# Two loads under way instead of four, a new instruction order, and 256-wide filling products in a fused RWKV-attention and SwiGLU kernel

## The chip, the cores and the metric

The kernel runs on one core of one Trainium2 chip. The metric is the device time in microseconds of one launch; the time before is the median of three runs. A profiled execution of the same kernel gives the rows that are quoted below. All times without a unit are microseconds, and those of the trace count from the first instruction of the span.

A core has a matrix engine (TensorE, called PE in the rows, with its weight loads as PEld), three engines for elementwise work (VectorE or DVE, ScalarE or ACT, GpSimd or POOL) and SyncE (SP), which in this kernel only issues transfers. An engine works through its instructions in the order in which they stand in its own queue; engines wait for each other by semaphores. TensorE is granted either its full clock or half of it, by a throttle that the profile shows as "PEclk".

## The reference

```python
batch, n_heads, seq, head_dim = (4, 8, 768, 48)
...
for t in range(S):
    kt, vt, rt = (k[:, :, t], v[:, :, t], r[:, :, t])
    cur = np.einsum('bhd,bhe->bhde', u[None] * kt, vt)
    y[:, :, t] = np.einsum('bhd,bhde->bhe', rt, state + cur)
    state = w[None, :, :, None] * state + np.einsum('bhd,bhe->bhde', kt, vt)
...
x = np.ascontiguousarray(attn_out.transpose(0, 2, 1, 3)).reshape(B * S, H * D)
...
rms = np.sqrt(np.mean(x * x, axis=-1, keepdims=True) + 1e-06)
xn = x / rms * rms_g
g = xn @ w_gate
silu = g * (1.0 / (1.0 + np.exp(-g)))
val = xn @ w_val
return (silu * val @ w_out).astype(np.float32)
```

So a linear attention with a decaying state runs over 768 positions for 4 batches of 8 heads of 48 channels, and its 3,072 rows of 384 go through a normalisation and a gated feed-forward layer of width 1,536. The three weight matrices arrive in 64-bit floating point, the rest in 32-bit.

## The kernel before

**Tiling.** The sequence is cut into 12 chunks of 64 positions. A chunk of all four batches is 256 tokens, called stage s (0 to 11). Each stage has a mixing part (attention) and a feed-forward part. Stages 0 and 1 go through the feed-forward layer one by one; from stage 2 on two stages share it, with seven products in place of eight (names f1 to f7, and P1 to P7 for the second layer).

**The names of the operations** (the number behind a name is the stage, and a half of the batches is called half 0 or half 1):

- On SP: *load k*, *load r* (stage 0's keys and receptances, one transfer for each half), *load chan* (both together, later stages, 1,024 KB), *load tok* (the same by tokens, 384 or 768 KB), *load v* (512 KB), *utab* (the bonus u, two transfers), *load 0* to *load 25* (pieces of the weights, 384 KB for the first six and 576 KB for the rest; 0 to 5 are the first quarter of gate and value weights, 6 to 17 the other three, 18 to 25 the output weights), *move* (heads 6 and 7 to their rows, two transfers), *store*, and *look* (the weights once more, for a check of their range).
- A piece of weights is rounded to 32 bits by four operations: *ulp* on ScalarE, *bits1* and *bits2* on VectorE, *sum* on GpSimd. There are six raw buffers and three of each intermediate one.
- On TensorE, for mixing: *E* (r by u times k: the bonus on the diagonal), *A* (r by k, decayed: the scores), *Y* (the outputs), *U* (the update of the state). These are many small products: E, A and U have 64 instructions each, Y has 128; in stage 0 they are done by halves (E and A 32, Y 48 instructions).
- Around them: *ku* (ScalarE, u times k), *R* and *K* (VectorE or GpSimd, r and k decayed), *d* and *m* (VectorE, the diagonal and the masked scores), *sq*, *yT* (ScalarE, squares and outputs), *yb* and *xb* (ScalarE, halves of yT or x exchanged between partitions), *gdup* and *wk* (tables of the decay, made once: gdup on ScalarE, then TensorE, then ScalarE), *h* (VectorE, decayed keys for U), *Rc* and *S*, *E* on ScalarE (copies for the state).
- The normalisation: *r* (TensorE, mean squares, in stages 0 and 1 products one column wide), *ms*, *inv*, *diag* (VectorE) and *pow* (GpSimd), *spread* (TensorE), *rms* (ScalarE), *x* (VectorE).
- The feed-forward part: *g s i o* is one of the two products for stage s, weight quarter i, block o; the first uses the gate-and-value array wa with yT or x, the second wb with yb or xb. Twelve instructions each. *silu*, *gv* and *hm* follow on ScalarE and VectorE; *P s i* is the second layer.

**The order.** All operations are added to a `Plan` (1,536 of them, each with an engine, an estimated cost and what it reads and writes). `ORDER`, a list of 1,536 numbers in the source, says in which order they are given out; `Plan.give` walks it, and each engine's queue follows from it. Dependencies become semaphore waits; the order decides who queues behind whom. `Plan.times` computes due times from the estimated costs, and `give` uses them for one thing: at a gap between TensorE operations it calls `warm(since, until)` with the two due times, and `warm` issues products of a matrix of ones that nobody reads, to fill the gap. A product in 32 bits is two instructions in the trace, with a weight load each.

**The loads under way.** Every input transfer on SP passes through `InOrder.at_most(n, give)`, which appends it to `flying` and, when more than n are in that list, makes the new one wait for the landing of the oldest. The limit is `IN_FLIGHT`, 4. `utab`, `move` and `store` don't pass through it; `look` has a list of its own with a limit of 1. Since SP's queue is in order, a load that waits, for the limit, for a raw buffer or for its target's last reader, holds everything behind it.

Of the kernel before, what the change touches and what calls it, by code (L numbers as in the profile page):

```python
# [49 lines left out]
P = 128  # L50
# [22 lines left out]
def feature_order():  # L73
# [10 lines left out]
    0, 6, 8, 42, 44, 5, 4, 7, 21, 11, 10, 41, 43, 16, 1, 2, 3, 45, 46, 47, 76, 12, 51, 48, 49, 52, 53, 55, 31, 36, 26,  # L84
    13, 14, 58, 50, 59, 15, 54, 17, 22, 60, 62, 65, 66, 100, 18, 19, 23, 24, 113, 9, 108, 103, 20, 67, 68, 83, 56, 27,
    61, 84, 63, 64, 57, 25, 69, 70, 38, 33, 39, 28, 71, 72, 124, 77, 86, 78, 126, 90, 29, 34, 118, 193, 85, 79, 87,
    30, 123, 80, 133, 32, 127, 125, 102, 81, 195, 82, 105, 106, 104, 37, 200, 128, 134, 35, 40, 107, 91, 131, 129,
    109, 114, 95, 130, 132, 92, 135, 119, 73, 110, 136, 96, 137, 155, 115, 111, 120, 116, 205, 210, 121, 139, 140, 97,
    138, 101, 93, 75, 74, 279, 112, 117, 141, 142, 143, 156, 150, 151, 157, 122, 98, 196, 163, 159, 160, 144, 197,
    198, 149, 145, 161, 206, 201, 164, 146, 199, 191, 274, 192, 284, 88, 152, 158, 162, 147, 148, 167, 218, 207, 202,  # L90
    165, 168, 169, 166, 203, 212, 213, 171, 172, 215, 170, 216, 208, 175, 176, 204, 209, 179, 180, 211, 177, 173, 217,
    174, 178, 183, 187, 89, 181, 182, 276, 219, 277, 153, 227, 275, 184, 188, 281, 194, 289, 280, 222, 282, 321, 311,
    306, 185, 225, 189, 247, 248, 249, 186, 214, 154, 190, 99, 278, 283, 251, 252, 255, 285, 250, 253, 254, 220, 256,
    257, 94, 238, 259, 263, 260, 264, 291, 286, 287, 288, 258, 267, 313, 308, 292, 314, 307, 224, 290, 228, 221, 271,
    316, 293, 261, 312, 268, 317, 265, 269, 223, 226, 309, 229, 331, 326, 336, 272, 266, 270, 262, 310, 315, 298, 302,
    294, 295, 242, 230, 322, 233, 234, 328, 355, 352, 318, 323, 299, 303, 296, 231, 300, 304, 297, 232, 353, 356, 235,
    236, 243, 327, 346, 319, 324, 305, 301, 329, 237, 244, 341, 273, 386, 390, 391, 387, 246, 354, 358, 245, 357, 320,
    325, 330, 332, 359, 362, 388, 392, 342, 333, 338, 334, 343, 344, 335, 339, 347, 337, 340, 345, 361, 364, 365, 348,
    360, 389, 375, 407, 349, 380, 363, 383, 381, 239, 393, 384, 500, 350, 366, 406, 394, 395, 351, 368, 369, 416, 437,
    367, 396, 241, 370, 501, 371, 382, 405, 404, 502, 398, 372, 399, 400, 373, 504, 503, 397, 438, 507, 509, 240, 374,  # L100
    376, 408, 378, 512, 377, 401, 402, 445, 409, 410, 385, 403, 413, 439, 446, 456, 457, 417, 441, 440, 447, 411, 442,
    462, 443, 444, 448, 451, 449, 463, 450, 464, 452, 453, 455, 454, 506, 458, 460, 465, 505, 459, 470, 467, 471, 466,
    468, 472, 508, 469, 473, 414, 415, 418, 590, 461, 422, 481, 474, 412, 476, 482, 510, 477, 478, 475, 483, 518, 591,
    513, 480, 484, 489, 485, 511, 479, 486, 490, 491, 487, 514, 488, 628, 492, 627, 519, 515, 520, 525, 493, 495, 624,
    526, 527, 496, 625, 497, 494, 521, 499, 528, 533, 523, 522, 530, 534, 419, 420, 423, 421, 424, 428, 524, 516, 517,
    425, 636, 529, 535, 498, 531, 544, 532, 626, 536, 634, 539, 598, 537, 545, 629, 540, 647, 541, 633, 538, 546, 543,
    547, 552, 635, 549, 548, 542, 550, 551, 630, 553, 631, 555, 554, 558, 632, 556, 563, 559, 560, 562, 565, 564, 557,
    567, 637, 426, 427, 429, 430, 566, 651, 568, 561, 571, 569, 570, 574, 582, 584, 575, 572, 573, 599, 577, 576, 578,
    638, 579, 434, 431, 583, 600, 595, 596, 601, 639, 581, 580, 592, 606, 585, 589, 593, 611, 432, 433, 588, 435, 586,
    602, 603, 587, 597, 436, 607, 642, 612, 643, 700, 640, 594, 747, 644, 701, 608, 615, 645, 756, 641, 652, 609, 610,  # L110
    646, 748, 614, 648, 649, 749, 616, 613, 617, 619, 618, 681, 744, 745, 650, 605, 653, 654, 621, 604, 682, 620, 657,
    746, 622, 683, 623, 660, 826, 689, 656, 684, 655, 685, 754, 690, 757, 753, 751, 691, 686, 706, 687, 688, 692, 695,
    693, 707, 708, 696, 697, 699, 709, 694, 702, 658, 703, 704, 714, 711, 698, 712, 715, 659, 661, 750, 662, 710, 663,
    705, 716, 717, 713, 725, 718, 755, 762, 719, 666, 720, 726, 827, 752, 727, 721, 723, 758, 722, 724, 728, 863, 733,
    860, 730, 664, 665, 763, 734, 729, 731, 732, 667, 669, 735, 736, 759, 760, 739, 864, 737, 769, 740, 771, 861, 741,
    770, 764, 765, 865, 743, 862, 772, 777, 866, 738, 766, 767, 670, 778, 668, 671, 774, 742, 773, 775, 780, 675, 779,
    776, 783, 834, 781, 867, 873, 782, 788, 784, 785, 790, 789, 835, 787, 791, 796, 793, 792, 786, 869, 797, 798, 794,
    795, 799, 802, 883, 800, 870, 676, 807, 803, 804, 806, 809, 808, 810, 801, 815, 812, 672, 673, 674, 677, 816, 768,
    761, 811, 805, 678, 888, 813, 818, 814, 821, 819, 817, 836, 831, 832, 871, 822, 823, 820, 872, 868, 825, 824, 828,
    829, 833, 874, 837, 843, 838, 679, 680, 844, 875, 839, 830, 878, 879, 847, 876, 841, 980, 981, 846, 877, 887, 880,  # L120
    842, 881, 845, 848, 851, 882, 884, 889, 886, 885, 984, 850, 891, 852, 890, 853, 919, 855, 849, 917, 918, 983, 920,
    982, 854, 856, 857, 990, 840, 858, 922, 921, 923, 924, 893, 859, 925, 892, 896, 931, 936, 926, 937, 927, 932, 933,
    928, 942, 929, 935, 944, 943, 945, 986, 938, 985, 939, 894, 930, 940, 934, 993, 895, 947, 950, 998, 987, 951, 946,
    948, 899, 1063, 941, 953, 952, 949, 954, 956, 961, 957, 1096, 958, 963, 962, 960, 964, 988, 992, 955, 965, 966,
    989, 969, 959, 967, 968, 972, 1097, 900, 897, 970, 898, 991, 975, 973, 976, 994, 901, 971, 1098, 905, 1001, 977,
    974, 979, 978, 999, 1005, 1000, 1007, 1006, 1003, 1013, 1008, 1002, 1010, 1009, 1011, 1012, 995, 1102, 1014, 1015,
    1070, 1016, 1019, 1017, 1105, 902, 903, 904, 908, 1062, 1024, 1020, 1021, 1119, 1023, 1026, 1025, 1027, 1018,
    1106, 1028, 1029, 1032, 1022, 1030, 1031, 1035, 1033, 1100, 1034, 1038, 1036, 1043, 1039, 906, 1103, 1040, 1045,
    1044, 1124, 1004, 1037, 909, 907, 911, 996, 1047, 1042, 1046, 1099, 1048, 1041, 1049, 1051, 1071, 1050, 1101,
    1109, 910, 1123, 1054, 1052, 1108, 1104, 1107, 997, 914, 1057, 1055, 1216, 1056, 1110, 1060, 1053, 1058, 1059,  # L130
    1061, 1064, 1072, 1111, 912, 1065, 1114, 1115, 1067, 1068, 1073, 1078, 1074, 1075, 1083, 1172, 1173, 913, 1069,
    1112, 1217, 1066, 1219, 915, 916, 1113, 1116, 1084, 1079, 1117, 1080, 1118, 1120, 1218, 1121, 1122, 1082, 1125,
    1126, 1087, 1229, 1076, 1088, 1086, 1089, 1091, 1085, 1155, 1127, 1153, 1154, 1077, 1128, 1156, 1093, 1094, 1158,
    1157, 1159, 1160, 1220, 1092, 1090, 1081, 1095, 1161, 1167, 1228, 1223, 1162, 1225, 1163, 1164, 1168, 1129, 1169,
    1226, 1165, 1171, 1174, 1221, 1234, 1177, 1299, 1178, 1132, 1180, 1298, 1166, 1222, 1179, 1175, 1176, 1186, 1170,
    1181, 1224, 1227, 1182, 1332, 1183, 1187, 1184, 1185, 1230, 1232, 1130, 1131, 1333, 1188, 1189, 1192, 1190, 1197,
    1193, 1135, 1335, 1194, 1199, 1198, 1235, 1191, 1196, 1200, 1205, 1195, 1202, 1203, 1133, 1134, 1206, 1201, 1138,
    1207, 1208, 1204, 1334, 1211, 1209, 1241, 1212, 1336, 1344, 1231, 1236, 1136, 1213, 1243, 1242, 1210, 1345, 1337,
    1237, 1215, 1244, 1214, 1249, 1238, 1239, 1246, 1245, 1250, 1251, 1247, 1248, 1137, 1139, 1140, 1144, 1252, 1255,
    1253, 1338, 1341, 1254, 1260, 1256, 1257, 1306, 1259, 1262, 1261, 1307, 1263, 1268, 1265, 1258, 1266, 1269, 1264,  # L140
# [18 lines left out]
class InOrder:  # L159


    def __init__(self, tc, engine):
        self.tc, self.engine, self.flying = tc, engine, []
# [87 lines left out]
def fast(ctx, tc, chan, tok, vpad, wka, wkb, wot, cols, u_row, out, bad):  # L251
# [12 lines left out]
    FIRST, IN_FLIGHT = 2, 4  # L264
# [25 lines left out]
    ones = c_tile([P, P], "ones")  # L290
# [85 lines left out]
    def load_chan(s):  # L376
        sp.at_most(IN_FLIGHT, lambda: sp.dma_start(out=CH, in_=chan[s]))
# [1479 lines left out]
```

## Time and profile before

| what | value |
|---|---|
| three runs | 595.24, 594.35, 594.51; median 594.51 |
| the profiled execution, its time | 594.61 |
| its span, first to last instruction | 592.9 |
| transfers | 62.97 MB, 22,766 packets; q1 (SP's) 61.36 MB, q8 (instructions) 0.95 MB in 58 packets |
| TensorE's waits before the tail | issue 1.7 (85.36) and 1.4 (13.49), VectorE 1.1 and 0.8, ScalarE 0.8 and 0.3, a transfer 0.6 |

In the rows of the chain of waits the columns are start, duration, engine and what it writes; "issue" is time in which the engine waited for nothing that the profile shows. All instructions stand on one line of the source, 179, since a helper emits them; so rows are told apart by the tile that is written (bank_a, bank_b, bank_c and at are the four accumulators).

The first 33 of the span are the head: stage 0's and stage 1's mixing with the first feed-forward products between them. TensorE's part of it, as the trace has it (start, name, instructions):

```
 1.15 fill x16          11.49 A 0 (half 0) x32    21.70 fill x4        28.61 A 1 x64
 5.25 E 0 (half 1) x32  12.07 fill x8             22.32 wk x4          29.70 g 0 0 1, wb x12
 5.87 fill x4           13.16 Y 0 x48             22.91 g 0 0 0, wb    31.10 g 0 0 2, wa x12
 6.86 E 0 (half 0) x32  15.71 r 0, r 0 x12        23.69 g 0 0 1, wa    32.49 Y 1 x128
 8.60 A 0 x32           17.14 g 0 0 0, wa, wa x24 24.98 g 0 0 0, wb    34.48 g 0 0 2, wb x12
 9.23 fill x12          19.47 fill x8             25.75 U 0 x64
10.76 Y 0 x48           21.27 spread 0 x2         26.72 E 1 x64
```

### The profile page before, as it was taken

The numbers are of one execution on the slowest core, as the hardware profiler recorded it, in microseconds if no ns is written. First come the engines' busy times: TensorE is split into PE (matmuls) and PEld (weight loads), VectorE is DVE, ScalarE is ACT, GpSimd is POOL, SyncE is SP. The second block draws the span as 40 slices with busy tenths as digits, with TensorE's granted clock in tenths as the row PEclk, the third lists the DMA queues.
The fourth block names the chain that finished last, engine by engine and source line by source line (L and its number), as shares of the span: only waits on it lengthen the run. The fifth ranks groups of instructions, "written<-read, shape, count | busy, mean of one in ns | idle before, by whom it ended". The sixth has DMA issues, their size and how long they took to land.

```text
span 592.9 us, 16578 instructions
## 1 busy us (share of the span) xinstructions
PE 581.5 (98%) x7270; PEld 517.2 (87%) x7270; DVE 416.3 (70%) x622; ACT 293.9 (50%) x713; POOL 41.7 (7%) x40
## 2 busy tenths in 40 slices
PE   7999989999999999999999999999999999999996
PEld 6888877667888999888899888899888899888896
DVE  7788768785786987786785676796766586355642
ACT  5774457374455744464373455594365482124100
POOL 3253234200000000000000000000000000000000
PEclk9899999999999999999999999999999999999999
DMA  8876462321415122523232335301441110301002
GB/s 276 303 249 264 158 248 83 126 61 54 154 65 166 55 74 73 181 84 97 81 92 54 92 108 200 117 24 30 137 157 46 52 63 12 96 3 54 1 4 54
DMA packets 22766, 62.97 MB, mean 106 GB/s; under 512 B 2944, under 2 KB 9760, under 8 KB 21280
## 3 DMA queue, kind: packets, MB, share of 16 engines
q1 hardware_dynamic: 21920, 61.36, 31.6%
q8 instruction: 58, 0.95, 0.7%
q10 hardware_dynamic: 768, 0.49, 0.3%
q14 instruction: 20, 0.16, 0.1%
HBM read 56.04 MB, written 4.72 MB: 102 GB/s over the span
## 4 chain that ended last, share of the span: by engine, by line
PE 96%; ACT 1%; issue 1%; DMA 1%; SPq 0%; DVE 0%; DVEq 0%
PE bank_b L179 33%; PE bank_a L179 27%; PE bank_c L179 27%; PE at L179 8%; DMA chan<-in_chan_dram 1%; ACT ku L179 0%; SPq L179 0%; ACT ST L179 0%; ACT wk L179 0%; DVE chan L179 0%; ACT RX L179 0%; ACT ulp L179 0%; ACT diag L179 0%; DVE rows_out L179 0%; DVE RR L179 0%
## 5 line engine op out<-in xcount | busy, mean ns | idle before, releaser
L179 DVE TENSOR_TENSOR gv<-bank_b,m 128x512 f32<-128x512 f32 x90 | 62.1, 690 | 61.3 <-PE bank_b L179 57.1
L179 ACT ACTIVATE gv<-gv 128x512 f32<-128x512 f32 (+1 forms) x60 | 30.8, 522 | 74.6 <-DVE gv L179 74.5
L179 PE MATMUL bank_b<-xa,wa 64*128 64x256 f32 x444 | 55.2, 379 | 1.7 <-issue 1.7
L179 DVE TENSOR_TENSOR gv<-bank_c,gv 128x512 f32<-128x512 f32 x60 | 41.4, 690 | 21.6 <-PE bank_c L179 21.1
L179 PEld LDWEIGHTS bank_b<-xa,wa 64*128 64x128 f32 x444 | 42.6, 187 | 7.6 <-issue 2.8
L179 PE MATMUL bank_a<-xb,wb 64*128 64x256 f32 x372 | 46.2, 379 | 0.0
L179 PE MATMUL bank_a<-xa,wa 64*128 64x256 f32 x372 | 45.6, 378 | 0.0
L179 PE MATMUL bank_a<-wo,h 128*128 128x192 f32 x264 | 45.2, 327 | 0.0
L179 ACT ACTIVATE MT<-dmask,du 128x64 f32<-128x64 f32 x160 | 41.9, 338 | 6.1 <-DVE du L179 6.0
L179 PE MATMUL bank_b<-t,s 64*128 64x256 f32 x360 | 44.4, 379 | 0.0
L179 PE MATMUL bank_b<-t,wb 64*128 64x256 f32 x360 | 44.2, 378 | 0.0
L179 PE MATMUL bank_c<-t,s 64*128 64x256 f32 x360 | 43.9, 376 | 0.0
L179 PE MATMUL bank_c<-xb,s 64*128 64x256 f32 x360 | 43.9, 376 | 0.0
L179 ACT COPY m<-bank_a 128x512 f32<-128x512 f32 (+1 forms) x35 | 19.9, 568 | 47.8 <-PE bank_a L179 39.1
L179 PEld LDWEIGHTS bank_a<-wo,h 128*128 128x128 f32 x264 | 43.2, 190 | 0.5
L179 ACT ACTIVATE gv<-bank_a 128x256 f32<-128x256 f32 x30 | 11.5, 382 | 57.5 <-PE bank_a L179 57.5
L179 PEld LDWEIGHTS bank_a<-xb,wb 64*128 64x128 f32 x372 | 35.7, 187 | 4.6 <-issue 0.3
L179 PEld LDWEIGHTS bank_a<-xa,wa 64*128 64x128 f32 x372 | 35.8, 187 | 4.2
L179 ACT ACTIVATE rows_out<-rows_out 128x384 f32<-128x384 f32 x72 | 39.1, 556 | 0.5
L179 PEld LDWEIGHTS bank_b<-t,s 64*128 64x128 f32 x360 | 34.4, 187 | 4.7 <-issue 0.7
L179 PEld LDWEIGHTS bank_c<-t,s 64*128 64x128 f32 x360 | 34.9, 187 | 4.0
L179 PEld LDWEIGHTS bank_c<-xb,s 64*128 64x128 f32 x360 | 34.9, 187 | 4.0
(189 smaller groups left out, 1099.0 us busy)
## 6 DMA issues: line engine op xcount, KB each, us to landing
chan<-in_chan_dram SPq DMA_DIRECT2D x11, 1024.0 KB, 5.5
TOK<-in_tok_dram SPq DMA_DIRECT2D x10, 768.0 KB, 4.8
V<-in_vpad_dram SPq DMA_DIRECT2D x12, 512.0 KB, 4.6
raw<-in_wot_dram SPq DMA_DIRECT2D x8, 576.0 KB, 5.5
rows_out<-in_wka_dram SPq DMA_DIRECT2D x12, 384.0 KB, 3.2
rows_out<-in_wkb_dram SPq DMA_DIRECT2D x12, 384.0 KB, 3.4
rows_out<-in_wot_dram SPq DMA_DIRECT2D x12, 384.0 KB, 3.1
raw<-in_wka_dram SPq DMA_DIRECT2D x6, 576.0 KB, 6.0
```

The lines of the kernel that those rows point to most:

```text
L179: return lambda *args, **kwargs: self.tc.keep_in_program_order(give(*args, **kwargs))
```

## The change

Three things are changed. First, the loads go through a method `load`, which counts them: the first thirteen keep the limit of four, from the fourteenth on it is two. `at_most` takes as many from the list as are over the limit. `look` keeps its limit of 1.

```diff
-        self.tc, self.engine, self.flying = tc, engine, []
+        self.tc, self.engine, self.flying, self.loads = tc, engine, [], 0
...
-        if len(flying) > n:
+        while len(flying) > n:
...
+    def load(self, out, in_):
+
+        self.loads += 1
+        return self.at_most(4 if self.loads <= 13 else 2, lambda: self.dma_start(out=out, in_=in_))
...
-        sp.at_most(IN_FLIGHT, lambda: sp.dma_start(out=CH, in_=chan[s]))
+        sp.load(out=CH, in_=chan[s])
```

The other loads (tok, v, the weight pieces, stage 0's k and r) are edited alike.

Second, the products that fill gaps are 256 columns wide in place of 128, other formulas give their number, and the list of accumulators that they write to has 14 entries in place of 12:

```diff
-    unused = list("baaaacbbbbbb")
+    unused = list("bbaaacbbbbbbbb")
...
-        bank = bank_of[unused.pop(0)]
-        if since < 2:
-            for _ in range(4 * int((until - 3.75) / 0.86)):
-                pe.matmul(bank[:, 0, 0:P], ones, ones, start=True, stop=True)
-        else:
-            for _ in range(int((until - since - 0.25) / 0.25)):
-                pe.matmul(bank[:, 0, 0:P], ones, ones, start=True, stop=True)
+        bank, wide_ones = bank_of[unused.pop(0)], free_dims(ones, (0, 2), (1, P))
+        for _ in range(int((until - 0.65) / 0.853) if since < 2 else int((until - since - 0.5) / 0.45)):
+            pe.matmul(bank[:, 0, 0 : 2 * P], ones, wide_ones, start=True, stop=True)
```

Third, `ORDER` is replaced by another permutation of the same 1,536 operations. The order of GpSimd's operations stays; those of the other four engines change from their first operations to their last. On TensorE, the first operations are:

```
before: E(half 1) E(half 0) A Y A Y r r g000wa g000wa spread wk g000wb g001wa g000wb U0 E1 A1 g001wb g002wa Y1 ...
after:  E(half 0) A E(half 1) Y A Y r r g000wa g000wa g000wb g000wb spread wk g001wa g001wb U0 E1 A1 g002wa Y1 ...
```

(g 0 0 0 is done by halves, so that it has four parts.) A 2 moves from the 50th place on TensorE to the 43rd, Y 2 from the 58th to the 46th, r 2 from the 65th to the 54th. On ScalarE, gdup moves from the third place to the fifteenth, just ahead of rms 0. On VectorE, K and R of half 0 come ahead of those of half 1. On SP:

```
before: k(1) r(1) k(0) r(0) load2 load0 v0 load1 load4 load5 load3 chan1 load8 tok0 load7 load6 load9 utab v1
        load10 load11 load12 load13 move1 tok1 load15 chan2 load14 tok2 load16 v2 load17 load21 load19 ...
after:  k(0) k(1) r(0) r(1) v0 load0 load1 load2 load3 chan1 load4 load5 tok0 | load6 load9 load7 v1 load8
        load10 utab load11 tok1 move1 load12 chan2 tok2 v2 load13 load14 load16 load15 load17 chan3 ...
```

The bar marks the fourteenth load. In the last operations the order on TensorE changes by one exchange (P7 and P3 of the last second layer), and those of stores by a few.

## The prediction

> **What bounds it now.** I read the busy shares first, then the chain of waits, TensorE's waits, and last the stretches that these point at. The page's first lines:
>
> ```profile
> span 592.9 us, 16578 instructions
> ...
> PE 581.5 (98%) x7270; PEld 517.2 (87%) x7270; DVE 416.3 (70%) x622; ACT 293.9 (50%) x713; POOL 41.7 (7%) x40
> ...
> DMA  8876462321415122523232335301441110301002
> ```
>
> TensorE is the bound, so time can come only from its idle stretches, its filling products and its half clock. The chain of waits, from its two stretches with idle time:
>
> ```profile
> 12.14 1.35 PE bank_c L179 x13
> 13.49 1.39 issue
> 14.88 0.90 PE bank_c L179 x37
> ...
> 21.90 0.37 ACT diag L179
> ...
> 28.61 1.16 PE at L179 x64
> ...
> 32.56 1.99 PE at L179 x128
> ...
> 85.36 1.67 issue
> 87.03 2.64 PE bank_b L179 x22
> ```
>
> From 29.7 on TensorE idles at one place before the tail, 85.36, where nothing that the profile shows is waited for; the order of products there is otherwise at its floor (12 instructions in 1.29). A move can thus pay before Y 1 (32.5) or at 85 only. The clock, by stretches (PE, PEld, DVE, ACT, POOL busy, then granted clock, DMA share, GB/s):
>
> ```profile
> 10.94:14.35 3.41, 2.55 (x93) 2.23 (x89) 3.12 (x9) 2.15 (x6) 1.36 (x2) 1.00 0.96 325
> 14.35:17.76 3.41, 2.88 (x65) 2.78 (x67) 1.21 (x2) 1.90 (x5) 0.83 (x2) 1.00 0.99 279
> 17.76:21.18 3.42, 3.42 (x26) 3.20 (x25) 2.74 (x9) 1.85 (x5) 1.47 (x2) 0.50 0.90 339
> ...
> 164.20:169.00 4.80, 4.80 (x156) 4.46 (x156) 4.66 (x6) 3.06 (x9) 0.00 (x0) 1.00 0.23 90
> ...
> 80.30:85.00 4.70, 4.70 (x155) 4.33 (x153) 1.55 (x4) 3.09 (x7) 1.54 (x2) 1.00 0.93 351
> ```
>
> The clock halves for one stretch of 3.4, after one that was 84% busy, but half of that with mean squares one column wide. The last two rows are two runs of Y's 128 dense instructions with what follows, some 155 each. The one beside a DMA share of 0.23 is followed by no idle, the one beside 0.93 by the idle 1.67. Queue q8 brings 58 packets of 16 KB to 14,540 TensorE instructions, 250 to a packet, so I take it to bring TensorE's own code. Between 72.9 and 84.6 its line is absent, in the next 1.1 it stands:
>
> ```profile
> q1 hardware_dynamic: 822, 3.95, 93.2%
> ...
> q8 instruction: 1, 0.02, 5.5%
> ```
>
> So the packet came late: behind the loads under way (four weight loads issued from 71.56 to 79.35, tok 3 at 79.39, which took 7.8). The idle at 13.49 has the same mark: no q8 packet in 7 to 12.5 (q1 95.5%), one in 12.5 to 13.6. Counting products, the first idle comes 221 weight-and-product pairs in, the second 1,152 = 9 x 128 later. A block is needed every 128 pairs.
>
> **The change, part by part.** Sums are against this execution's 594.6 (span 592.9 and 1.7 around it); the median is 594.5.
>
> *Two under way.* At 85 the late packet cost the product there 1.94 (3.24 between starts against 1.30), and r 2 behind it 0.30, waiting for ScalarE's yT 2. In the new order Y 2 stands some 16 earlier, at about 64; chan 3 waits for A 2 just ahead of it, so when its block is asked for one or two loads are under way. I take the whole 2.24 as gained; bounds -2.24 and 0, and +1.9 if another dense run is hit instead.
>
> The Trainium skill (DMA: Bandwidth & Descriptors, Queues, rings and completion order) says that an engine goes round the queues it has work for after each packet. By it a code packet would wait for one data packet whatever is under way, and the limit would bring nothing: about 595.2 with the terms below. The missing q8 line speaks against it.
>
> What two can cost: from 28.00 to 32.49 four moved 341 GB/s, a lone V of 512 KB (at 98.14) took 3.7 and a lone chan of 1,024 KB (at 104.61) 5.4, so about 2.0 of a load is latency and two of 576 KB together take about 5.4. V 1 waits for U 0's read, as before (26.98), but loads 8, 10, utab, 11 and tok 1 now queue behind it. Load 8 leaves at 27.5, not 15.46, and lands near 32. Conversion (0.73 ScalarE, 0.45 and 0.75 VectorE, up to 1.79 GpSimd, in turn behind 7) ends by 39.5; its first product stands at about 40. Cover 0.5 to 1; gone, each us is a us. Load 13 moves from 35.25 to about 48, behind move 1, chan 2, tok 2 and V 2; landed at 52 and rounded by 58, wanted at 68. Cost taken 0, bound +1.
>
> *Filling products.* The branch for the first gap now gives 6 of 256 columns in place of 8 of 128; later gaps have 1 and 1 for 2, 6, 4, 4, 2 (counts from the planner's own due times; the trace has x16, 4, 12, 8, 8, 4, two instructions each). The first sixteen, from 1.15, took 3.46, so 0.21 each; 12 twice as wide take 5.1 at that pace, done at 6.3, or at 5.3 if the pace doubles at 4.1, as the starts of the last few show. The first E now waits for r's first half, third to land (6.08), so about 6.2: covered, bound +0.2.
>
> *The head, in the new order.* K and R of half 0 come first: K from 6.0 (0.68), R beside GpSimd's K (1.12 in the same company before), A at 8.0 against 8.60; the second E behind it, Y at 10.2 (10.76), A at 10.9, second Y at 12.6 (13.16). That 0.6 runs into the code block. Before the second Y the new stream has 12+32+32+32+2+48+32+2 = 192 pairs, so it stops at its 30th pair of 48 until the block lands. The block was usable at 14.88; asked for after as many pairs it is asked about 1.3 later, behind loads that land at 13.3 in place of 12.1: 14.9 to 16.1. I take 15.6, and Y done at 15.9 (15.78 before).
>
> Then two mean squares (1.5), and four products ahead of spread where there were two. The last pair waits for yb (3.6 after Y: 19.5) and takes 2 x 0.77, or 2 x 1.43 at the half clock (as the second part of g 0 0 0 did from 18.04): spread at 21.0 to 22.3, against 21.27, where it had stood behind filling products (diag was ready at 20.36). If 10.94 to 14.35, now some 1.5 busy, loses the clock from 14.35, the mean squares take 2.6: spread at 22.8. gdup (1.26), moved ahead of rms on ScalarE, ends 5.5 after Y, at 21.4, and is covered unless spread comes before 20.8. Spread: +0.5, bounds -0.3 and +1.5.
>
> The Trainium skill (TensorE: Matmul & The Clock Gate, Why this matters for your kernels) has the clock fall only after idle gaps of over about 3 us. By it fewer fillers are free and the head gains 0.3, for 592.4; the clock rows show a fall with no such gap.
>
> From rms to A 1 the chain is ScalarE's: ku, wk, ku, RX, ulp, ST, 21.90 to 28.61. The new order has the same six, so it moves as a whole. g 0 0 1's second half (1.30), moved ahead of U, leaves the stretch between A 1 and Y 1, but Y 1 waits for masked scores (VectorE until 32.34): TensorE waits some 1 there instead. Worth 0, or -0.2 by VectorE's small swaps, taken. Head: +0.3, bounds -1.0 and +1.5.
>
> *Later order.* The same products, at the floor; 80 turns between row modes for 78. An ordinary product beside a turn took 1.40 for 1.30, and two dense ones stretch alike: +0.3, bounds 0 and 0.5. VectorE is 70% busy; its conversions are ahead of need by the 10 above.
>
> Sum: -2.2 + 0.3 + 0.3 = -1.6: **593.0**.
>
> **Rivals.** (1) *The half clock and the first block eat the gain.* Head at +1.5: 594.6 - 2.2 + 1.5 + 0.3 = 594.2. For: 1.5 busy where 2.55 was; four products before spread. Against: the phase of those 3.4 stretches is unknown. (2) *The limit does not lift the idle,* or it comes back elsewhere once: 594.6 + 0.3 + 0.3 - 0.3 (r 2's wait, gone all the same) = 594.9. For: utab and moves are outside the count; a short window at A 1 (block wanted 19 pairs into it, entered in U). Against: 164 shows that a quiet queue suffices. (3) *Slower: dense runs outrun the code.* Between 26 and 34 U, E, A and Y 1 take 320 pairs, with V 1 and load 8 sent together at 27 as blocks are wanted 19 pairs into A 1 and 71 into Y 1. Each miss costs 1.4 to 1.9. One in all is rival 2; from the second on (or one with the head at its bound) it is slower: 594.9 + 1.65 = 596.5. For: blocks need two or three us there. Against: before, at share 0.97 from 28.00 to 32.49, none missed.
>
> **How the numbers follow.** Forecast 0.46; (1) 0.22 and (2) 0.12, both within 0.2% (1.2, about what this kernel's measurement can tell from no change: 593.3 to 595.7); (3) 0.20. So faster 0.46, same 0.34, slower 0.20. The forecast's own range: 591.7 (head at -1.0) to 593.3. For 8 in 10 it takes in (1), (2) and part of (3): 591.8 to 595.6.
>
> **What would show it.** No idle of 1.67 after Y 2 and none in its place; second Y begun near 12.6 and stopped midway; spread between 21.0 and 22.8; Y 1 within 1 of 32.5 with an idle before it; loads from the fourteenth on landing in 3.5 to 5.5. It is wrong if TensorE waits for POOL's sums (loads 8, 13), if "issue" idles stand after A 1 or Y 1, or if the clock stays halved past 21.2.

## The result, and the profile after

| | median | lowest to highest | runs |
|---|---|---|---|
| before, beside it | 594.51 | 593.40 to 597.51 | 19 |
| after | 597.70 | 594.30 to 600.98 | 19 |

The ratio is 1.005 [1.0031, 1.0069]: slower by half a per cent, outside the range of 591.8 to 595.6, and on the side that had a chance of 0.20. The times also spread over 6.7, where those of before spread over 4.1. The profiled execution took 599.24, 1.5 over the median; its rows are read against before's profiled 594.61. A count such as x17 is of TensorE's multiplications; a product in 32 bits is two of them, each with a weight load. First the page and TensorE's waits (waited for: total, times, longest):

```profile
span 597.5 us, 16511 instructions
...
PE 583.8 (98%) x7234; PEld 515.4 (86%) x7234; DVE 415.7 (70%) x622; ACT 294.2 (49%) x713; POOL 43.3 (7%) x40
...
PE at L184 <- issue: 3.9, 2, 2.3
PE bank_c L184 <- issue: 1.6, 1, 1.6
PE bank_b L184 <- DVE h L184: 1.1, 1, 1.1
```

"issue" was 3.1 before (1.7 and 1.4); it is 5.5 now. So the idle at 85 has gone, but two others of the same kind have come. The chain of waits says where (start, duration, what; the columns as before):

```profile
28.44 0.50 PE at L184 x17
28.94 2.28 issue
31.22 1.55 PE at L184 x47
32.77 2.86 PE bank_c L184 x12
35.63 2.66 PE at L184 x128
38.29 1.50 PE bank_c L184 x12
...
68.89 1.99 PE at L184 x128
70.88 1.50 PE bank_b L184 x12
...
385.73 1.98 PE at L184 x126
387.71 1.65 issue
389.36 0.27 PE at L184 x2
```

A 1 (x17, then x47) stops after 17 of its 64 multiplications for 2.28. The twelve of g 0 0 2 then take 2.86, where 1.29 to 1.50 is usual, and Y 1 takes 2.66 for 1.99. Y 2 (68.89) now runs into what follows without idle. Y 9 stops for 1.65, two multiplications from its end. The windows show the clock around the first stop (TensorE's busy time is the second number, the granted clock the one behind the last bracket):

```profile
26.85:30.26 3.41, 1.45 (x81) 1.23 (x74) 3.38 (x5) 3.24 (x6) 2.33 (x3) 1.00 0.76 244
30.26:33.67 3.41, 2.45 (x51) 2.20 (x52) 0.79 (x3) 0.72 (x1) 1.17 (x1) 0.50 0.74 211
33.67:37.09 3.42, 3.42 (x66) 2.55 (x66) 3.39 (x6) 0.73 (x1) 0.00 (x0) 0.50 0.70 243
37.09:40.50 3.41, 3.41 (x106) 3.11 (x100) 1.92 (x4) 2.14 (x5) 1.98 (x2) 1.00 0.77 264
```

A window with 1.45 of 3.41 busy is followed by one at half clock, and that one, 2.45 busy, by another. The Trainium skill (TensorE: Matmul & The Clock Gate, Why this matters for your kernels) puts the fall behind idle gaps of over about 3 us; here the longest gap was 2.28, and two windows of 3.4 ran at 0.50.

The queues, first from 24.9 to 28.9, then from 28.9 to 30.1 (packets, MB, share):

```profile
q1 hardware_dynamic: 248, 0.99, 82.4%
...
q1 hardware_dynamic: 86, 0.31, 65.6%
q8 instruction: 1, 0.02, 4.9%
```

It is the mark that stood at 85 before: no packet of code for 4, then one (at 28.97), and 2.2 later TensorE goes on.

The account of this execution: A 1 begins at 28.44 (28.61 before), so the head up to there gained 0.2. Y 1 begins at 35.63 (32.56), and the product behind it at 38.29 (34.55), so 3.7 are lost by then. The gap at 85 gives back 2.2, and Y 9 costs 1.9 with its restart. That makes 3.4 of the 4.6 by which the span grew; the other 1.2 lie in small differences along the way.

### The profile page after: what moved, and what is told of

Same layout as the page of the kernel before. It is cut to its first block, busy times and chain, and to the rows that moved or that the text cites. A ratio compares the mean times of both kernels' runs of the same rounds, so it can differ in the third digit from the quotient of the medians.

```text
span 597.5 us, 16511 instructions
## 1 busy us (share of the span) xinstructions
PE 583.8 (98%) x7234; PEld 515.4 (86%) x7234; DVE 415.7 (70%) x622; ACT 294.2 (49%) x713; POOL 43.3 (7%) x40
## 4 chain that ended last, share of the span: by engine, by line
PE 93%; DMA 3%; DVE 1%; issue 1%; ACT 0%; POOL 0%; SPq 0%; DVEq 0%; ACTq 0%
PE bank_b L184 32%; PE bank_a L184 26%; PE bank_c L184 26%; PE at L184 8%; DMA TOK<-in_tok_dram 1%; DMA raw<-in_wka_dram 1%; DMA raw<-in_wkb_dram 1%; DMA chan<-in_chan_dram 1%; DVE ms L184 0%; DVE bits L184 0%; DVE KH L184 0%; POOL ms L184 0%; ACT ST L184 0%; SPq L184 0%; DVE diag L184 0%
## 5 line engine op out<-in xcount | busy, mean ns | idle before, releaser
L184 ACT ACTIVATE gv<-gv 128x256 f32<-128x256 f32 (+1 forms) x60 | 30.9, 522 | 67.0 <-DVE gv L184 66.2
L184 PEld LDWEIGHTS bank_a<-xa,wa 64*128 64x128 f32 x372 | 35.4, 187 | 4.7 <-issue 0.5
```

The source lines that it names most:

```text
L184: return lambda *args, **kwargs: self.tc.keep_in_program_order(give(*args, **kwargs))
```

## The experiments

**What was on trial.** Theory, called late code: TensorE gets its instructions in blocks of 256, and a block that is asked for behind loads under way comes late; where TensorE stops is set by how many instructions stand ahead. Rivals: the limit of two starves the loads; the new order itself is worse; the wide filling products cost by themselves. "Ratio" is to the kernel before, run beside it on the same chip (medians of 594.78 to 595.15); "after + 48" is the changed kernel with 48 instructions more.

| kernel | median | range | runs | ratio [95%] |
|---|---|---|---|---|
| limit alone | 597.42 | 593.39 to 598.89 | 6 | 1.0045 [1.0030, 1.0061] |
| fillers alone | 595.65 | 594.33 to 596.97 | 11 | 1.0011 [0.9999, 1.0024] |
| order alone | 596.44 | 593.55 to 599.74 | 12 | 1.0023 [1.0003, 1.0043] |
| fillers undone | 595.26 | 593.77 to 597.06 | 12 | 1.0008 [0.9995, 1.0020] |
| limit undone | 600.04 | 595.00 to 601.15 | 9 | 1.0061 [1.0035, 1.0087] |
| order undone | 598.25 | 595.30 to 600.42 | 12 | 1.0053 [1.0035, 1.0071] |
| limit from the 21st load | 595.09 | 591.96 to 598.73 | 12 | 1.0006 [0.9984, 1.0028] |
| after + 132 | 603.72 | 601.65 to 609.85 | 5 | 1.0139 [1.0123, 1.0155] |
| after + 132, one load at the end | 602.87 | 600.37 to 605.51 | 6 | 1.0130 [1.0100, 1.0159] |
| after + 192 | 597.28 | 594.76 to 603.67 | 12 | 1.0047 [1.0023, 1.0070] |
| after + 40 | 594.50 | 593.39 to 596.08 | 12 | 0.9981 [0.9969, 0.9992] |
| after + 48 | 592.68 | 591.73 to 593.99 | 7 | 0.9957 [0.9939, 0.9974] |
| after + 56 | 594.59 | 592.72 to 597.18 | 12 | 0.9989 [0.9969, 1.0010] |
| fillers undone, + 8 | 594.76 | 593.79 to 597.43 | 12 | 0.9993 [0.9976, 1.0010] |
| after + 48, limit undone | 594.35 | 592.25 to 597.36 | 12 | 0.9991 [0.9974, 1.0008] |
| before + 56 | 602.74 | 599.65 to 604.32 | 6 | 1.0116 [1.0093, 1.0140] |

### The three parts, alone and undone

Each kernel takes one part of the diff into the kernel before, or one part back out of the changed one. Its lines are those of the change; the undone limit is one line:

```diff
-        return self.at_most(4 if self.loads <= 13 else 2, lambda: self.dma_start(out=out, in_=in_))
+        return self.at_most(4, lambda: self.dma_start(out=out, in_=in_))
```

> The kernel before with the limit of two from the fourteenth load as its only edit; TensorE's stream of instructions is unchanged. Late code (TensorE gets its instructions in blocks of 256, and a block comes late when loads are under way and the products ahead of it are dense; the place of a stop is set by the count of instructions): the stop of 1.67 at 85 is gone or under 0.5, the one of 1.4 in stage 0's second Y stays, nothing new; 592.3 (591.8 to 593.2). The limit starves the loads: TensorE waits for rounded weights or V, 596 or more. The order or the fillers alone made the loss: 592.5 to 594.5, which does not tell them from late code.

> The kernel before with the wide filling products as its only edit: 15 products, so 60 instructions, fewer ahead of A 1. Late code: the block that was wanted in stage 1's E, A with slack is now wanted 60 instructions later, in A 1, within 3.3 us of its request, so a new stop of 1.5 to 2.3 stands in A 1 between 26 and 29, and the stop at 85 moves or goes; 594.6 to 596.5. The fillers or their clock alone made the whole loss: 597 or more. The order made it: 594.5 within 0.5, the stop at 85 as before and none in A 1.

> The kernel before with the new order as its only edit: four loads under way and narrow fillers, 19 of them ahead of A 1 where the changed kernel has 8, so 44 instructions more. Late code: no stop in A 1 and none in Y 9 at 387; with four under way one stop of about 1.7 may stand at some dense run below 110; 592.5 to 594.8. The order itself made the loss: 597 or more, with A 1 to Y 1 as late as in the changed kernel.

> The changed kernel with the narrow fillers of before: limit and order stay, 11 more products, so 44 instructions more, ahead of A 1. Late code: the block wanted in A 1 is asked for 5.2 us ahead, so the stop of 2.28 there is gone or under 0.6, the one of 1.65 at 387 too, and the half clock from 30 to 37 with them; Y 1 begins near 32.5; 592.6 (591.8 to 593.6). The limit or the order made the loss: 596.5 to 598. The wide fillers made it by their clock, not by their count: about 593 to 594.5 too, but then a count of 48 more with wide fillers stays at 597.

> The changed kernel with four loads under way throughout; order, wide fillers and TensorE's stream stay. Late code: the block in A 1 is as late or later, the stop there 2 or more with the half clock behind it, and a stop in Y 2 may come back: 597.5 to 600. The limit made the loss (V 1 or pieces held back): 594 to 595.5, with the stop in A 1 gone.

> The changed kernel with the order of before: limit and wide fillers stay, 12 instructions more ahead of A 1. Late code: blocks as in the kernel with the wide fillers alone, a stop of 1 to 2 in A 1 or Y 1 and none at 85, and V 1 held back by the limit as in the kernel with the limit alone: 596 to 598. The order made the loss: 592.5 to 594.5.

The parts don't add up, so no part is the cause by itself. Into the new order with its limit, the wide fillers bring 2.4 (595.26 to 597.70); into the kernel before, 0.7, which its interval does not tell from nothing. The limit costs 2.5 in the old order, where late code had given a gain (592.3). In the changed kernel the medians have it gain 2.3 (600.04 to 597.70), but the intervals of the two ratios overlap (1.0061 and 1.0050), so that gain is not shown. The fillers alone fit late code: in A 1 (29.2, for 0.6) and Y 1 (34.4, for 1.1) there are new stops, at 85 none. The order alone (596.44) missed both theories, since late code had given 592.5 to 594.8; it has no stop in A 1 or Y 9, but one of 1.8 in Y 1. Undoing the fillers missed by 2.7: the stop in A 1 shrank to 1.1 and moved into E 1, and the one at 387 and the half clock from 30 to 37 are gone. Undoing the order left the time where it was (598.25); its profiled execution has no stop for code over 0.4, where late code had one of 1 to 2.

Undoing the limit shows more. Y 2 of the changed kernel, with four loads under way throughout:

```profile
70.78 1.99 PE at L184 x128
72.77 1.50 PE bank_b L184 x12
```

The idle of 85 is gone there too, and so it is with the order alone and with the fillers alone, both with four loads. So in the changed kernel it did not need the limit.

The limit alone also showed the rival in part. TensorE's waits there, and with the order undone, in the profiled executions:

```profile
PE bank_b L184 <- DVE h L184: 1.7, 2, 1.1
PE at L184 <- DMA V<-in_vpad_dram: 1.5, 1, 1.5
PE at L184 <- DVE chan L184: 0.9, 1, 0.9
```

```profile
PE at L184 <- DVE bits L184: 2.5, 2, 1.4
PE bank_b L184 <- DVE h L184: 2.4, 2, 1.3
```

With the limit in the old order V 1 leaves at 28.40 and lands at 32.79, where it left at 26.98 and landed at 30.22; Y 1 starts at 32.82. And with limit and wide fillers in the old order TensorE waits for VectorE's conversions (bits). Is V 1 all of it? In one more kernel the limit starts later:

```diff
-        return self.at_most(4 if self.loads <= 13 else 2, lambda: self.dma_start(out=out, in_=in_))
+        return self.at_most(4 if self.loads <= 20 else 2, lambda: self.dma_start(out=out, in_=in_))
```

> The kernel before with the limit of two from the twenty-first load on, in place of the fourteenth; V 1 (the seventeenth) and the loads ahead of it keep four. If the limit costs by V 1, which it holds back until 28.4 and lands at 32.8, just as Y 1 wants it: V 1 lands by 31, Y 1 never waits for it, the stop at 85 stays away, 592.3 to 593.5, and the runs scatter as little as those of the kernel before. If it costs by weight pieces that come late after 35, or by later loads: 596 or more, as the limit alone. If the limit alone was slow for another reason than the loads, as many slow runs as there.

> The limit alone once more, for the profile of another execution (its timed runs lay at 596.0 to 598.9, its first profiled one at 593.4). V 1 held back: Y 1 begins 2 to 5 later than 32.8, with V landing just ahead of it and no half clock. Late code: stops of 1 to 2.5 at an instruction that is 193 more than a multiple of 256, in A 1 or Y 1.

Four loads up to the twentieth took back 2.3 of the 2.5, as the theory of the early loads has it; but V 1 landed at 33.09 there too, so its own landing is not shown to be the cause, and the runs still spread from 592.0 to 598.7. A second profiled execution of the limit alone took 593.14 with no stop of TensorE for code; the first (593.39) has one of 0.3. So neither profile shows what cost its five other runs (596.04 to 598.89), and that stays open. The clock does not explain it: the granted clock of these five is 0.993 to 0.999, and 0.999 in the slowest.

### The count of instructions by itself

The direct test: the changed kernel, with small products in place of some wide ones in the first gap, where TensorE waits for its first load. A product is four instructions, two weight loads and two multiplications, so n small ones for m wide ones shift all that follows by 4(n - m). Little else changes: the fillers of this gap can also end later, and the first E with them, at 6.62 with +132, 7.40 with +48 and 8.90 with +192, where it was 6.51. For +132 (n 36, m 3):

```diff
-        for _ in range(int((until - 0.65) / 0.853) if since < 2 else int((until - since - 0.5) / 0.45)):
+        for n in range(36 if since < 2 else 0):
+            a = 64 * (n % 2)
+            pe.matmul(
+                bank_of["a"][a : a + 64, 1, 0:L], ones[a : a + D, 0:L], ones[a : a + D, 0:L], start=True, stop=True,
+                skip_group_check=True,
+            )
+        for _ in range(3 if since < 2 else int((until - since - 0.5) / 0.45)):
```

> The changed kernel with 36 small products in place of three of the six wide ones in the first gap: 132 instructions more, all of them where TensorE waits for its first load anyway. Late code: the blocks of the head are asked for 6.9, 8.1, 9.3, 6.6 and 6.1 us ahead of need, so the stops in stage 0's second Y and in A 1 are gone or under 0.5, the half clock from 30 to 37 too, and the one at 387; a block is wanted 2.2 us after its request at about 350, so a new stop of 1 to 2 stands there; Y 1 begins before 33; 593.5 (592.5 to 595). Limit, order, fillers' clock: these stay as they were, 597 to 598.

> The same with 52 small products in place of four wide ones: 192 instructions more. Late code: no stop in stage 0's second Y; the fourth block is asked for 3.5 us ahead of need, between 24 and 28, so a stop of 2 to 3 stands in U, E 1 or ahead of A 1, and one of 1 to 2 at 350 (2.2 us ahead); none at 387; 596 (594.5 to 598). The other theories: 597 to 598, with the stops where the changed kernel has them.

> The changed kernel with 13 small products in place of one of the six wide ones in the first gap: 48 instructions more, all before TensorE's first load has landed. Late code, as the runs so far sharpen it (a block starts to move when the loads that were under way as it was asked for have landed, 4 to 6.5 us in the worst cases): with 48 more no block that is wanted early is asked for behind a fresh load but the first, so the stop of 1.6 in stage 0's second Y stays, those in A 1 (2.28) and at 387 (1.65) are gone, and the half clock that followed the one in A 1: 594.0 (592.8 to 595.5), with less scatter. Limit, order, or the wide fillers' clock as the cause: 597 to 598, as the changed kernel.

After + 132 lost 6 more (603.72) where late code had foretold a gain: the sign was wrong, but the rivals named had left the time at 597 to 598. Its chain of waits and its queues (436.9 to 443.3, then 443.3 to 444.5) in the profiled execution of 609.85:

```profile
439.75 1.98 PE at L184 x127
441.73 4.08 issue
445.81 0.34 PE at L184
```

```profile
q1 hardware_dynamic: 218, 1.42, 61.4%
...
q8 instruction: 1, 0.02, 4.9%
q1 hardware_dynamic: 2, 0.00, 0.1%
```

Here the loads are few: tok (issued at 433.2) and chan (436.2, landed 443.8), two, and the block was asked for near 436.8 (when TensorE began the instruction 304 ahead of the one that stops; why 304, the last section says). 218 packets of data go first, then the code at 443.4, then two packets more: it moved when the load ahead of it was all but done, 6.6 after it was asked for, and Y 10 stood one multiplication from its end for 4.08. I had reckoned with the time between request and need only, not with what a single load of 1,024 KB does to it. With that added (a block starts to move about when the loads that were under way at its request have landed) the worst and best counts change places: + 132 bad, + 48 to 56 good. The expectation for + 48 was written from that, and it held, 0.1 under its range: 592.68, faster than before and 5.0 under the changed kernel. + 192 fell within its range, but also into that of the other theories (597 to 598); the places tell them apart: the stops in stage 0's second Y and at 387 are gone, that in A 1 is 0.5, and one of 4.1 stands in Y 1, where the changed kernel has none. (Its fillers also ran on to 8.5, past the first loads.) TensorE's waits with + 48:

```profile
PE at L184 <- DMA V<-in_vpad_dram: 1.2, 1, 1.2
...
PE bank_c L184 <- issue: 0.5, 1, 0.5
```

The first block still stops stage 0's second Y, by 0.5; the 3.9 of A 1 and Y 9 are gone, and no window from 7.74 to 38.46 ran at half clock. The next one did, with no stop ahead of it, behind one that was 3.36 of 3.41 busy, 1.95 of that with stage 1's mean squares:

```profile
35.05:38.46 3.41, 3.36 (x30) 2.86 (x29) 1.57 (x4) 3.35 (x6) 2.55 (x2) 1.00 0.88 286
38.46:41.87 3.41, 3.41 (x20) 2.77 (x18) 2.68 (x6) 1.34 (x6) 2.74 (x3) 0.50 0.83 239
```

That the load under way holds the block was then tested at 441 alone:

```diff
-        return self.at_most(4 if self.loads <= 13 else 2, lambda: self.dma_start(out=out, in_=in_))
+        return self.at_most(4 if self.loads <= 13 else 2 if self.loads <= 61 else 1, lambda: self.dma_start(out=out, in_=in_))
```

> The kernel with 132 instructions more (603.72), with a limit of one load from the sixty-second on: stage 10's V, tok and chan go one after the other. TensorE's stream stays. There a block was asked for at 437.0, just after tok (433.2) and chan (436.2, 1,024 KB, landed 443.8) had been issued; it began to move at 443.4, and TensorE stood for 4.1 from 441.5. Late code behind the loads under way: tok is issued near 436.1 and chan near 439.5, after the request, so the block moves at about 439 and the stop at 441 is under 1, and the half clock from 445 is gone: 598 to 600.5. If the stop there has nothing to do with the load under way: it stays, 602 to 605.

```profile
437.57 2.15 PE at L184 x128
439.71 1.50 PE bank_b L184 x12
```

Y 10 now runs through. Tok left at 433.99 and chan at 438.16, after the request (434.6); the code moved at 437.28, 0.8 before tok landed. So the place behaves as foretold, in one execution. The median fell by 0.9 only (602.87), short of the 598 to 600.5 that I had given: the 4.1 belonged to the slowest of five runs of + 132, and most of what + 132 loses lies elsewhere (in this profile a stop of 2.7 at 34, one of 0.5 at 73 and one of 0.9 at 359). By the time alone the edit did nothing: the ratios, 1.0130 and 1.0139, lie within each other's intervals.

### Is it the count, or a draw?

Neighbours of + 48, the limit undone at that count, and the same shift in the kernel before (20 small products for six of its eight narrow ones):

> The changed kernel with 11 small products in place of 13, so 40 instructions more in place of 48 (592.68). Late code: the third block is asked for at 20.1, behind the wait for spread, and not at 18.7, so it has 5.4 in place of 6.7 and comes late by 0.5 to 1.5, in A 1: 593.9 (593.0 to 595.5). If only the two small products (0.2 of time in the first gap) count: 592.7 within 0.5.

> The changed kernel with narrow fillers (595.26) and two more of them in the first gap: 8 instructions more, 52 more than the changed kernel; 0.4 of work where TensorE waits for a load. Late code: the third block is now asked for at about 19.6, ahead of the wait for spread, and not at 21.4 behind it, so it has 7.0 until its need in place of 5.4 to 5.7, and the stop of 1.4 in E 1 goes: 593.2 (592.2 to 594.3). If the narrow fillers or their places cost the 2.6 to the kernel with 48 more and wide ones: 595.3 within 0.7.

> The changed kernel with 15 small products, 56 instructions more. Late code: the third block is asked for ahead of the wait for spread as with 48 more (592.68), with 7.1 to its need, and no other block of a dense run comes behind a fresh load, so the same time within 0.8: 592.0 to 593.5, and no stop of over 0.7 but the one in stage 0's second Y. If 592.68 was a lucky draw among kernels that differ by a few small products, as 594.50 with 40 more may say: 594 to 595.

> The kernel with 48 instructions more (592.68) with four loads under way throughout. Late code: with four under way a block waits longer, and blocks three and four are asked for behind fresh loads again: stops of 1 to 2.2 in E 1 or A 1 and up to 1 in Y 1: 596 (594 to 598.5). If the limit is worth only what it took from the stop at 85: 592.7 to 594.

> The kernel before with 20 small products in place of six of its eight narrow ones in the first gap: 56 instructions more, in about the same time. Late code: the blocks that are wanted in dense runs just behind fresh loads are now others: stops of 2 to 3.5 near 430, 1 to 2.7 near 82, about 1.4 each near 350 and 33: 600 (597 to 603), so the same shift that gained 5 in the changed kernel loses 5 here. If small products or a longer first gap gain by themselves: 592 to 594.8.

Before + 56 is the clearest: 20 small products, in a gap where TensorE waits, cost an unchanged order, limit and weight stream 7.6. Its waits:

```profile
PE bank_c L179 <- issue: 4.1, 3, 1.9
...
PE at L179 <- issue: 1.1, 1, 1.1
```

Three stand about where they were expected, at 35.4, 84.8 and 356.1, and one at 455.0. Near 430 TensorE waits 1.2 at 437.3, at the place of a block too, but the profile puts that wait down to VectorE's h. The four sum to 5.2, where before's two sum to 3.1; the span of this execution is 5.5 longer, so 3.4 of it are not placed.

The neighbours came out between: + 40 at 594.50 (inside its range, but its profile has no stop in A 1; Y 1 waits 2.1 for V 1 instead), + 56 at 594.59 and narrow fillers + 8 at 594.76, both above theirs. In the last two the block in stage 0's second Y stopped TensorE for 2.3 and 2.0, and three windows and one of half clock followed in the head; nothing stopped for code afterwards, which was foretold. So all four counts from + 40 to + 56 lose the stops in A 1 and Y 9 and gain 2.9 to 5.0 on the changed kernel. That + 48 is 1.8 or more better than its neighbours is not explained; the intervals of their ratios overlap, + 56 came out where a lucky draw of + 48 would have it (594 to 595), and in the profile of + 48 the first stop was the smallest of them. Four loads at + 48 cost 1.7, within the range that late code gave: a stop of 1.4 in Y 1 comes back.

Late code gave a range for 16 kernels. Five medians lie in it, three within 0.3 of it and eight outside. So it tells where TensorE stops better than what a kernel takes.

Where the stops stand is the strongest evidence. Count TensorE's multiplications, its weight loads and the 51 other instructions in its queue (waits for semaphores for the most part, which the page does not count as busy) together, from 0. Then in the 19 profiles every wait of TensorE for "issue" of over 0.3 ahead of the tail, 36 in all, ends at an instruction that is 193 more than a multiple of 256. Five kernels as examples:

| kernel | instruction (start of the wait) |
|---|---|
| before | 449 (13.49), 2753 (85.36) |
| after | 449 (13.18), 961 (28.94), 10433 (387.71) |
| after + 132 | 449 (11.32), 1473 (36.75), 2497 (75.55), 9665 (361.12), 11713 (441.73) |
| before + 56 | 1473 (35.45), 2753 (84.78), 9665 (356.07), 12225 (454.97) |
| after + 48 | 449 (12.97) |

## Why the prediction was wrong, point by point

- *Two under way takes the idle at 85: -2.24.* Right in the profiled executions: no idle behind Y 2. But that was luck in part: with four loads under way the changed kernel has none there either. And the reason was too wide. I had taken two loads for few enough; the block at 441 waited 6.6 behind two, and in after the one for A 1 waited 4.2 behind two (asked for near 24.8, moved at 28.97).
- *Filling products: covered, bound +0.2.* **The step that failed.** I priced them by their microseconds alone, and there they are indeed covered: E 0 begins at 6.51. But the change gives 18 products fewer by the end of the head, so 72 instructions fewer, and all later blocks fall elsewhere; the stops that this brings stood at nothing in the sum and only in rival 3. In the profiled execution they cost 3.7 by 38.29 and 1.9 in Y 9. With narrow fillers the same kernel takes 595.26; with 48 instructions more in its first gap, 592.68. So by these two kernels the term was +2.4 to +5.0, not 0.
- *Rival 3, dense runs outrun the code, chance 0.20.* The place was right (wanted 19 pairs into A 1, stopped after 17 multiplications), the price near: 2.28 and 1.65, against 1.4 to 1.9 each. What spoke against it, that none was missed from 28.00 to 32.49 in the kernel before, held for that count only. It also lacked the half clock behind the stop (about 2.2 between 32.77 and 38.29). Its sum, 596.5, is the nearest of the four to 597.70.
- *The head: +0.3.* Second Y begun at 12.24 (12.6 foretold), stopped after 29 multiplications (in its 30th pair), done at 15.35 (15.9), spread at 21.23 (21.0 to 22.8), A 1 at 28.44. Right, up to A 1. One reading of it was rough: the 1,152 pairs between the two idles of before are 1,148 pairs and eight other instructions of TensorE's queue, so a block is 256 of all its instructions and not 128 pairs.
- *What two can cost: 0, bound +1.* No wait for the rounded pieces in the changed kernel; loads from the fourteenth to the twenty-first took 3.75 to 5.44, as foretold, though load 8 left at 29.45, 2.0 later than I had it. V 1 landed at 32.07, which would have held Y 1 near 32.4 had the stop not. With the old order the same limit cost 2.5.
- *Later order: +0.3.* Not told apart; 1.2 of the span's growth is unplaced.
- *The range.* It ended at 595.6, since I had given a second stop and the clock behind it less than 2 in 10.

The rule from the Trainium skill that I had weighed (DMA: Bandwidth & Descriptors, Queues, rings and completion order) had code wait for one data packet and the limit bring nothing. At 437 it waited for 218 of the profile's, some 14 to each of the 16 engines. The page counts typically 9 to 17 descriptors to a packet; if that is what the profile lists, 14 are one packet and the rule stands, but my reading of it, a short wait whatever is under way, does not. No run here shows which. A page that I did not weigh bears on it: the Trainium skill (Runtime: NRT & Kernel Launch, Instruction fetch mechanics) has code refilled in 16 KiB blocks of 256 instructions, which these runs confirm (57 packets of 16 KB in the changed kernel, stops multiples of 256 apart). It calls the crossing mostly hidden; here it cost up to 4.08 at one place.

## What to carry to other kernels

Where "issue" idles stand at instruction numbers that differ by a multiple of the code block (256 here), count instructions, not only time: any edit of the count ahead, even of products that nobody reads, moves every later stop. Look which loads are issued just ahead of a dense run, and keep large ones from leaving as its next block is asked for. Before two versions are compared, try each at a few counts: here 132 instructions in the first gap were worth more (6.0) than the change itself (3.2).

## What was not expected of the hardware

- A code block seems to be asked for some 304 instructions ahead of its need (in quiet stretches its packet moves about 1 after instruction 145 + 256 j begins, and TensorE stops at 449 + 256 j; the request itself has no row, so each time of a request here is an estimate from this). Y's 128 multiplications with their weight loads, 256 instructions and so one whole block, take 1.99.
- It then starts to move up to 6.6 later, the longest ones with loads under way, and TensorE goes on 2.2 to 2.6 after it starts in most cases (up to 3.6, with + 192).
- Each of the six stops of over 2.2 had the half clock begin during it or 0.1 behind it; of the seventeen from 1.0 to 2.0, eleven had none within 3.4 behind them. The half clock also came without a stop for code ahead of it (at 7.8 with the fillers undone, at 38.5 with + 48). Times vary from run to run: after, + 132 and + 192 spread over 6.7 to 8.9, + 48 over 2.3 (7 runs). That the stops vary with them is not shown, since most kernels have one profile.
